# Where two experts' first y tiles and rest rows are scaled out, in a kernel of linear attention and routed experts

## The chip, the cores and the metric

The kernel runs on one core of a Trainium2 chip. The time is device microseconds of one execution, from 3 runs. TensorE multiplies matrices into PSUM (eight banks of 128 x 512 fp32); VectorE and ScalarE do the elementwise work and empty PSUM; SyncE (SP) and ScalarE issue DMAs. Every engine carries out its own list of instructions strictly in order and waits for the others by semaphores.

## The reference

Random-feature linear attention gives x (2304 rows of 512). Each row is sent to one of 8 experts, a two-layer net, and its result is weighted.

```python
q_p, k_p = phi(q_s), phi(k_s)                    # exp of random features
kv = np.einsum('bhsm,bhsd->bhmd', k_p, v)
out = (q_p @ kv) / den                           # -> x, N = 2304, D = 512
logits = x @ w_gate                              # E = 8 experts, F = 1024
expert_idx = np.argmax(logits, axis=1)
gate_w = probs[np.arange(N), expert_idx]
...                                              # rows gathered by expert, at most `capacity`
h = np.maximum(np.einsum('ecd,edf->ecf', disp, w1), 0.0)
y = np.einsum('ecf,efd->ecd', h, w2)
out[i] = gate_w[i] * y[expert_idx[i], pos[i]]
```

## The kernel before

The attention comes first, then the routing, then the experts. The rows lie in four blocks of 576; `item(j)` takes the j-th expert pass over such a block (line 1215). Passes 1 to 3 stand behind branches (line 1443) that are taken only if so many are needed: with these inputs passes 0, 1 and 2 run. "The second expert" below is pass 1, "the third" pass 2 and "the fourth" pass 3, which is prepared but does not run.

Every fp32 product is made of three: each operand is split in a high part (fp32r) and a low part (the remainder), and TensorE adds high x high, low x high and high x low. `split_w_hi` and `hi_part` are casts on ScalarE (line 151), `split_w_lo` and `lo_part` differences on VectorE (line 154). `turn_x` transposes a part of x on VectorE (line 489), and casts and splits it (lines 494, 495).

A pass has two stages. The first makes h = relu(x w1). The second, `second` (`second_late` in the third expert), makes y = h w2 in four tiles of 128 rows and one group of 64 rest rows. A tile is 24 matmuls of 128 x 512: 16 with the high half of w2 (`upper`, lines 1012 and 1013) and 8 with the low half (`lower`, line 1018); the rest rows (line 1022) are 16. The tiles 0 and 2 use PSUM bank 3, the tiles 1 and 3 bank 4, so the fourth tile can only begin when the second has been scaled out of its bank. `second` yields tile 0, the rest rows, tile 1, tile 2, tile 3; `second_late` yields tile 0, tile 1, the rest rows, tile 2, tile 3. After each `yield`, `item` writes what `prep` names for that number n, then `finish`: a scaling by the gate weight on ScalarE (line 1067) into one of three buffers `y`, and the store to the output. For the rest rows it first copies half of the bank on ScalarE (line 1064) and adds the other half on VectorE (line 1065). Stores are issued by SyncE, that of the last tile by ScalarE; each store to the output waits for the one before.

The third expert (`SEVEN`) makes its first stage by seven products of quarters in place of eight (Strassen's scheme in Winograd's form). It needs sums of quarters of w1 (S1 to S4) and of x (T1 to T4), made on VectorE (`sum_part`, line 1114), each split again in high and low. `PREP` names which of this is written into the tail of the second expert, at which n; `BETWEEN` names what is written between the products. The products use, in this order, (A11, B11), (A12, B21), (S2, T2), (S1, T1), (S3, T3), (S4, B22), (A22, T4). S1 and S2 lie in turn in one buffer (`w_sum`); T1 and T2 share one as well.

The order of each engine's list is the order in which this code is written; no scheduler changes it.

Of the kernel before, what the change touches and what calls it, by code (L numbers as in the profile page):

```python
# [29 lines left out]
NB, NBA = SLOTS // 32, 8  # L30
# [28 lines left out]
SEVEN = 2  # L59
# [8 lines left out]
def attention_moe(ctx, tc, kT, qT, va, om, wg, w1, w2, cap, ident, tri, desc, lst, tab0, out):  # L68
# [78 lines left out]
    def split_hi(hi, raw, eng=None):  # L147
        if eng is nc.gpsimd:
            nc.gpsimd.tensor_scalar(hi, raw, 1.0, 1.0, op0=ALU.mult, op1=ALU.mult)
        else:  # L150
            nc.scalar.copy(hi, raw)  # L151

    def split_lo(lo, raw, hi, eng=None):
        (eng or nc.vector).tensor_tensor(lo, raw, hi.bitcast(F32), op=ALU.subtract)  # L154
# [295 lines left out]
    def load_w(i, c, ev, chunks_of="(p k)"):  # L450
        if i == 1:
            f = c // 2 * (FF // 2)
            src = w1[ds(ev, 1), :, f : f + FF // 2].rearrange(f"o {chunks_of} f -> p (o k) f", p=128)
            src = src[:, c % 2 * 2 : c % 2 * 2 + 2, :]
        else:
            src = w2[ds(ev, 1), c * 256 : (c + 1) * 256, :].rearrange("o (k p) f -> p (o k) f", p=128)
        nc.sync.dma_start(w_raw[i][c], src)

    def split_w_hi(i, c, eng=None):
        split_hi(w_hi[i][c], w_raw[i][c], eng)  # L460

    def split_w_lo(i, c, eng=nc.vector, k=None):
        sl, cs = slice(None), slice(None)
        if k is not None:
            sl, cs = slice(k // 2, k // 2 + 1), slice(k % 2 * 256, k % 2 * 256 + 256)
        split_lo(w_lo[i][c][:, sl, cs], w_raw[i][c][:, sl, cs], w_hi[i][c][:, sl, cs], eng)
# [14 lines left out]
    def load_x(rows, b0=0, b1=NB, qs=range(4)):  # L481
        src = x_d[rows, :].rearrange("(b r) (q c) -> q r b c", r=32, q=4)
        for q in qs:
            nc.sync.dma_start(big["xz"][32 * q : 32 * q + 32, b0:b1, :], src[q])


    def turn_x(b0, b1, o=0, eng=nc.vector):
        t = big["xt"][:, o : o + b1 - b0, :].rearrange("p b (k r) -> p b k r", k=4)
        nc.vector.transpose(t, big["xz"][:, b0:b1, :].rearrange("p b (a k) -> p b k a", k=4))
        t = t.rearrange("p b k r -> p k b r")  # L490
        hi, lo = (big[x][:, :, 32 * b0 : 32 * b1].rearrange("p k (b r) -> p k b r", r=32) for x in ("xhi", "xlo"))

        def split():
            nc.scalar.copy(hi, t)
            eng.tensor_tensor(lo, t, hi.bitcast(F32), op=ALU.subtract)

        return split
# [285 lines left out]
    def mm1(f, n, hhi, hlo, hr, nm):  # L783
        xhi, xlo = big["xhi"], big["xlo"]
        fs = slice((f % 4) * 128, (f % 4) * 128 + 128)
        a, z = HALVES[n]
        sl = slice(a, z)
        pt = bank(turn[0] % 3, f"h{nm}{f}{n}")[:, 0 : z - a]
        turn[0] += 1
        for k in range(4):  # L790
            whi_, wlo_ = (w[1][f // 4 * 2 + k // 2][:, k % 2, fs] for w in (w_hi, w_lo))
            nc.tensor.matmul(pt, whi_, xhi[:, k, sl], start=(k == 0), stop=False)  # L792
            nc.tensor.matmul(pt, wlo_, xhi[:, k, sl], start=False, stop=False)  # L793
            nc.tensor.matmul(pt, whi_, xlo[:, k, sl], start=False, stop=(k == 3))  # L794

        def take():
            w = min(z, 4 * SUB) - a
            sl = slice(a, a + w)
            parts = [(hhi[:, f, sl], hlo[:, f, sl], pt[:, 0:w])]
            if n == 1:  # L800
                parts.append((hr[:, f, 0:REST], hr[:, f, REST:], pt[:, w:]))
            for hi, lo, src in parts:
                nc.scalar.activation(hi, src, AF.Relu)  # L803
            for hi, lo, src in parts:
                nc.vector.scalar_tensor_tensor(lo, src, 0.0, hi.bitcast(F32), op0=ALU.max, op1=ALU.subtract)  # L805

        return take
# [77 lines left out]
    for n in range(NK + NT + 3):  # L885
# [9 lines left out]
        elif t < NT:  # L895
            pj = [bank((2 * t + i) % 3, f"pjq{n}{i}") for i in range(2)]
            c = max(i for i in range(len(QB) - 1) if QB[i] <= t)
# [307 lines left out]
    def listing(n):  # L1205
        stop[0] = None
        for _ in range(n):
            if stop[0] is None:
                stop[0] = next(il, 0)
                if stop[0] == 0:  # L1210
                    return
# [3 lines left out]
    def item(j):  # L1215
        nonlocal row, row_a
        nm = f"i{j}"
        last = j == B - 1
        hhi, hlo, hr = h0
        if j > 0:  # L1220
            row_a = nc.scalar.value_load(resd[0:1, 1, j - 1 : j], min_val=0, max_val=N - S)
        out_j = [out[0:SLOTS, :]] * 2 if j == 0 else [out[ds(r, SLOTS), :] for r in (row, row_a)]
        sc = sc_b[:, 0, :] if j == 0 else sc_j[:, j - 1, :]

        def put(i, n, y, out_j=out_j):

            k = int(i == NSUB - 2)
            (nc.sync, nc.scalar)[k].dma_start(out_j[k][i * SUB : i * SUB + n, :], y[0:n, :])

        def addresses():  # L1230
            nonlocal row
            ev = nc.sync.value_load(resd[0:1, 0, j : j + 1], min_val=0, max_val=E - 1)
            row = nc.sync.value_load(resd[0:1, 1, j : j + 1], min_val=0, max_val=N - S)
            evs.append(ev)
            load_x(ds(row, SLOTS))

        def weights():
            for c in range(4):
                load_w(1, c, evs[-1])

        def between(p):
            if p == 1:
                for c in range(4):
                    load_w(2, c, evs[-1])
                addresses()
            for f, *a in BETWEEN.get(p, ()):
                f(*a)
            for c in LOADS.get(p, ()):
                load_w(1, c, evs[-1])

        if j == SEVEN:
            seven(hhi, hlo, hr, nm, between)
        for k, (f, half) in enumerate(STEPS[j > 0] if j != SEVEN else ()):
            mm1(f, half, hhi, hlo, hr, nm)()
            if j == 0:
                listing(5 if k > 4 else 1)
            if 0 < j < B - 1 and k == 0:
                for c in range(4):
                    load_w(2, c, evs[-1])
            if 0 < j and not last and k == 4:  # L1260
                addresses()
                weights()
            if j == 0 and k < 3:
                zero_out(k)
            if half == 0:
                continue
            for i, c in HI_AT[j > 0].get(f, ()):
                split_w_hi(i, c)
            for i, c in LO_AT[j > 0].get(f, ()):
                split_w_lo(i, c)  # L1270
        if j == 0:
            for _ in il:
                pass
            addresses()
            weights()

        def ready(c):
            split_w_hi(1, c)
            split_w_lo(1, c)

        if 0 < j != SEVEN - 1 and not last:
            turn_x(0, NBA)()
            ready(0)
            turn_x(NBA, NB)()
            ready(1)
        if j == B - 2:
            for c in range(4):
                load_w(2, c, evs[-1])
        prep = PREP if j == SEVEN - 1 else {}
        parts = second_late if j == SEVEN else second  # L1290
        for n, (i, pt) in enumerate(parts(hhi, hlo, hr, nm)):
            first_x = turn_x(0, NBA) if j == 0 and n == 1 else None
            for f, *a in prep.get(n, ()):
                f(*a)
            finish(i, pt, nm, sc[:, i : i + 1], put)
            if first_x is not None:
                first_x()
            yield

            if j == 0 and n == 2:  # L1300
                ready(0)
                last_x = turn_x(NBA, NB)
                ready(1)
                last_x()

    def turns(*qs):
        return [(turn_part, q) for q in qs]

    def sums(*qs):
        return [(sum_part, q) for q in qs]  # L1310

    def his(*qs):
        return [(hi_part, q) for q in qs]

    def los(*qs):
        return [(lo_part, q) for q in qs]

    PREP = {
        0: [
            *turns("B11", "B21"), *his("B11", "B21", "A11"), *turns("B12", "B22"), *sums("T1"), *his("T1", "A12"),  # L1320
            *los("B11", "B21", "A11", "A12"), *sums("S1"), *his("S1"), *los("T1"),
        ],
        1: [*sums("T2"), *his("T2"), *los("T2", "S1"), *sums("S2"), *his("S2"), *los("S2"), *sums("S3", "T3", "S4", "T4")],
    }
    BETWEEN = {
        1: [*his("S3", "T3"), *los("S3", "T3")],
# [73 lines left out]


    first = item(0)
    for k in range(BRANCH_AT):
        next(first)
# [98 lines left out]
```

## Time and profile before

| | us |
|---|---|
| median of 3 runs | 268.0 (267.24 to 269.23) |
| profiled execution, whole | 268.11 |
| its span, first to last instruction | 266.3 |
| TensorE busy in the span | 250.7 (94%) |
| VectorE, ScalarE busy | 181.5, 152.5 |
| mean granted clock of TensorE | 0.981 |

The whole time of the profiled execution is 1.8 us above its span. Matmuls are pipelined, so a row's own duration is longer than the distance to the next matmul's start; distances of starts are what counts. Times in the rows are from the span's start.

### The profile page before, as it was taken

What the parts mean: (1) busy time and instruction counts of PE and PEld (TensorE: products, weight loads), DVE (VectorE), ACT (ScalarE), POOL (GpSimd) and SP (SyncE); (2) the same over time, 40 slices, a digit from 0 to 9 for tenths busy, and PEclk for the clock granted to TensorE, in tenths of its full rate; (3) what the DMA queues carried; (4) which work ended last, traced back from release to release, by engine and by line L of the source; (5) the groups of instructions that cost most, each with busy time, mean ns of one, the idle gap of its engine ahead of it and who ended that gap; (6) DMA issues with size and microseconds to landing.
All of it is one profiled execution on the core that took longest, in us unless ns stands there. A gap on an engine that the chain in (4) does not pass through costs nothing. (4 is left out here: it accounts for less than half of the span.)

```text
span 266.3 us, 7692 instructions
## 1 busy us (share of the span) xinstructions
PE 250.7 (94%) x3026; PEld 229.2 (86%) x3026; DVE 181.5 (68%) x385; ACT 152.5 (57%) x383; POOL 52.1 (20%) x102
## 2 busy tenths in 40 slices
PE   8899999999999999999999999999957999999593
PEld 7799898999999999999888899998836999987482
DVE  3988987688899997556836555669880097798400
ACT  4878777899999973256016355534322379703611
POOL 1043212345799964000000000000000000000000
PEclk9999999999999999999999999999995999999799
DMA  6997979326997466920395189900102999062221
GB/s 234 410 304 243 352 254 330 112 100 183 271 259 262 165 206 236 378 74 1 102 287 212 51 278 237 330 6 2 39 0 89 299 248 311 1 214 104 81 62 43
DMA packets 33412, 49.07 MB, mean 184 GB/s; under 512 B 2578, under 2 KB 16530, under 8 KB 33362
## 3 DMA queue, kind: packets, MB, share of 16 engines
q1 hardware_dynamic: 32242, 46.91, 55.9%
q10 hardware_dynamic: 1120, 1.52, 1.7%
q8 instruction: 28, 0.46, 0.7%
q14 instruction: 22, 0.18, 0.2%
HBM read 36.49 MB, written 11.93 MB: 182 GB/s over the span
## 5 line engine op out<-in xcount | busy, mean ns | idle before, releaser
L1012 PE MATMUL yi<-w2hi,hhi 128*128 128x512 f32 x96 | 39.9, 416 | 7.8 <-ACT ysi L1067 7.8
L1013 PE MATMUL yi<-w2hi,hlo 128*128 128x512 f32 x96 | 39.6, 412 | 0.0
L792 PE MATMUL hi<-xhi,w1hi 128*128 128x256 f32 (+1 forms) x128 | 37.8, 295 | 0.0
L793 PE MATMUL hi<-xhi,w1lo 128*128 128x256 f32 (+1 forms) x128 | 37.5, 293 | 0.0
L794 PE MATMUL hi<-xlo,w1hi 128*128 128x256 f32 (+1 forms) x128 | 37.5, 293 | 0.0
L1012 PEld LDWEIGHTS yi<-w2hi,hhi 128*128 128x128 f32 x96 | 19.4, 202 | 12.9 <-ACT ysi L1067 8.7
L805 DVE SCALAR_TENSOR_TENSOR hlo<-hi,hhi 128x256 fp32r<-128x256 f32 x32 | 13.4, 419 | 21.5 <-ACT hr L803 13.9
L206 DVE TENSOR_REDUCE mx<-pjk 128x4 f32<-128x512 f32 (+1 forms) x38 | 23.3, 654 | 4.5 <-PE pjk L189 3.2
L803 ACT ACTIVATE hhi<-hi 128x256 fp32r<-128x256 f32 x32 | 12.2, 386 | 23.9 <-PE hi L794 23.9
L792 PEld LDWEIGHTS hi<-xhi,w1hi 128*128 128x128 f32 x128 | 24.0, 188 | 0.6 <-PE hi L794 0.3
L154 DVE TENSOR_TENSOR w1lo<-w1raw,w1hi 128x1024 fp32r<-128x1024 f32 x11 | 13.3, 1218 | 16.1 <-ACT w1hi L151 16.1
L793 PEld LDWEIGHTS hi<-xhi,w1lo 128*128 128x128 f32 x128 | 24.0, 188 | 0.0
L794 PEld LDWEIGHTS hi<-xlo,w1hi 128*128 128x128 f32 x128 | 24.0, 187 | 0.0
L1018 PE MATMUL yi<-w2lo,hhi 128*128 128x512 f32 x96 | 23.6, 389 | 0.0
L853 ACT ACTIVATE ex<-pjk,mx 128x128 f32<-128x128 f32 x72 | 20.7, 372 | 4.1 <-DVE mx L206 3.4
L1013 PEld LDWEIGHTS yi<-w2hi,hlo 128*128 128x128 f32 x96 | 19.4, 202 | 4.1
L739 PE MATMUL qacc<-kv_sb,qpT 128*64 128x73 f32 x576 | 22.5, 229 | 0.1
L289 PE MATMUL kacc<-v,ex 128*64 128x65 f32 (+1 forms) x576 | 21.4, 230 | 0.7 <-issue 0.7
L1018 PEld LDWEIGHTS yi<-w2lo,hhi 128*128 128x128 f32 x96 | 18.0, 188 | 3.8
L961 ACT ACTIVATE d<-pjq,mx 128x128 f32<-128x128 f32 x72 | 21.1, 411 | 0.2 <-DVE mx L206 0.2
L189 PE MATMUL pjk<-om_s,kraw 64*128 64x128 f32 x288 | 20.4, 284 | 0.8 <-PE pjk L189 0.7
L289 PEld LDWEIGHTS kacc<-v,ex 128*64 128x64 f32 x576 | 19.4, 137 | 2.0 <-issue 1.1
(210 smaller groups left out, 542.7 us busy)
## 6 DMA issues: line engine op xcount, KB each, us to landing
w1raw<-w SPq DMA_DIRECT2D x16, 512.0 KB, 7.0
w2raw<-w SPq DMA_DIRECT2D x16, 512.0 KB, 4.6
x_d<-xr SPq DMA_DIRECT2D x18, 256.0 KB, 3.3
xg<-x_d SPq DMA_DIRECT2D x12, 288.0 KB, 6.1
v<-va SPq DMA_DIRECT2D x8, 325.0 KB, 4.8
kraw<-kT SPq DMA_DIRECT2D x8, 288.0 KB, 4.5
out<-ysi SPq DMA_DIRECT2D x9, 256.0 KB, 2.2
v<-va SPq DMA_DIRECT2D x3, 650.0 KB, 7.2
```

The lines of the kernel that those rows point to most:

```text
L189: nc.tensor.matmul(banks[i][:, k * M : (k + 1) * M], parts[k][rows, :], om_s[rows, :], start=True, stop=True)
L206: nc.vector.tensor_reduce(mx[:, a : a + src.shape[1]], src, op=ALU.max, axis=AX.X, negate=True)
L289: nc.tensor.matmul(acc[f : f + 64, i * 2 * VW + o : i * 2 * VW + o + (z - a) * VW], ex[:, 4 * i + k, f : f + 64], v[:, i, a * VW : z * VW] ...
L739: nc.tensor.matmul(acc[i][r : r + 64, p * ROW : (p + 1) * ROW], qpT[:, r // 64, (4 * i + p) * 64 : (4 * i + p) * 64 + 64], kv_sb[(t * 128 ...
L792: nc.tensor.matmul(pt, whi_, xhi[:, k, sl], start=(k == 0), stop=False)
L793: nc.tensor.matmul(pt, wlo_, xhi[:, k, sl], start=False, stop=False)
L794: nc.tensor.matmul(pt, whi_, xlo[:, k, sl], start=False, stop=(k == 3))
L853: nc.scalar.activation(ex[:, o + k, :], q[:, k * M : (k + 1) * M], AF.Exp, bias=mx[:, o + k : o + k + 1], scale=1.0)
L961: nc.scalar.activation(d[:, 4 + k, :], pj[1][:, k * M : (k + 1) * M], AF.Identity, bias=mx[:, 4 + k : 5 + k], scale=1.0)
L1012: nc.tensor.matmul(pt, hhi[:, f, sl], w2_at(w_hi, f), start=(f == 0), stop=False)
L1013: nc.tensor.matmul(pt, hlo[:, f, sl], w2_at(w_hi, f), start=False, stop=False)
L1018: nc.tensor.matmul(pt, hhi[:, f, sl], w2_at(w_lo, f), start=False, stop=(f == 7))
```

## The change

No instruction is added or taken away. Their order is changed at the ends of the second and the third expert. In the second, S2 and the sums S3, T3, T4 and S4 are written behind the rest rows and the second y tile (n = 3 in place of n = 1), and S1's low half ahead of T2's casts. In the third, the two parts of x and of w1 for the fourth expert were written ahead of all y tiles; they now stand ahead of the rest rows (n = 2) and of the third y tile (n = 3), so that the first two tiles are scaled first.

```diff
@@ -1278,15 +1278,10 @@
             split_w_hi(1, c)
             split_w_lo(1, c)
 
-        if 0 < j != SEVEN - 1 and not last:
-            turn_x(0, NBA)()
-            ready(0)
-            turn_x(NBA, NB)()
-            ready(1)
         if j == B - 2:
             for c in range(4):
                 load_w(2, c, evs[-1])
-        prep = PREP if j == SEVEN - 1 else {}
+        prep = {SEVEN - 1: PREP, SEVEN: STANDARD}.get(j, {})
         parts = second_late if j == SEVEN else second
         for n, (i, pt) in enumerate(parts(hhi, hlo, hr, nm)):
             first_x = turn_x(0, NBA) if j == 0 and n == 1 else None
@@ -1315,12 +1310,21 @@
     def los(*qs):
         return [(lo_part, q) for q in qs]
 
+    def ready_x(*b):
+        turn_x(*b)()
+
+    def ready_w(c):
+        split_w_hi(1, c)
+        split_w_lo(1, c)
+
+    STANDARD = {2: [(ready_x, 0, NBA), (ready_w, 0)], 3: [(ready_x, NBA, NB), (ready_w, 1)]}
     PREP = {
         0: [
             *turns("B11", "B21"), *his("B11", "B21", "A11"), *turns("B12", "B22"), *sums("T1"), *his("T1", "A12"),
-            *los("B11", "B21", "A11", "A12"), *sums("S1"), *his("S1"), *los("T1"),
+            *los("B11", "B21", "A11", "A12"), *sums("S1"), *los("T1"), *his("S1"),
         ],
-        1: [*sums("T2"), *his("T2"), *los("T2", "S1"), *sums("S2"), *his("S2"), *los("S2"), *sums("S3", "T3", "S4", "T4")],
+        1: [*sums("T2"), *los("S1"), *his("T2"), *los("T2")],
+        3: [*sums("S2", "S3"), *his("S2"), *sums("T3", "T4"), *los("S2"), *sums("S4")],
     }
     BETWEEN = {
         1: [*his("S3", "T3"), *los("S3", "T3")],
```

ScalarE, the tail of the second expert, one piece of the difference (`ysi_8719` is its first scaled y tile, `yi1r` the bank of the rest rows, `yi_8653` that of the second tile, `w1hi_1079` here S2's high part):
```order
 L1067 ACTIVATE ysi_8719<-yi_8651,sc_j 128x512
 L151 CAST xhi<-x_more 128x576
+L1064 COPY ysi_8734<-yi1r 64x512
+L1067 ACTIVATE ysi_8734<-ysi_8734,sc_j 64x512
+L1067 ACTIVATE ysi_8747<-yi_8653,sc_j 128x512
 L151 CAST w1hi_1079<-w_sum 128x1024
-L1064 COPY ysi_8741<-yi1r 64x512
-L1067 ACTIVATE ysi_8741<-ysi_8741,sc_j 64x512
-L1067 ACTIVATE ysi_8754<-yi_8653,sc_j 128x512
-L1067 ACTIVATE ysi_8782<-yi_8757,sc_j 128x512
+L1067 ACTIVATE ysi_8782<-yi_8750,sc_j 128x512
 L1067 ACTIVATE ysi_8810<-yi_8785,sc_j 128x512
```
The cast of S2 moves from ahead of the rest rows to behind the second y tile; the two y rows after it differ in a buffer's number alone.

VectorE, the same tail, before, from T2's low half on (`w1lo_1084` is S1's low part, `w1lo_1083` S2's; `w1raw_1075` becomes S3, `x_more` T3, `w1raw_1074` S4, `xt` T4):
```order
L154 TENSOR_TENSOR xlo<-x_more,xhi 128x576
L154 TENSOR_TENSOR w1lo_1084<-w_sum,w1hi_1080 128x1024
L1114 TENSOR_TENSOR w_sum<-w_sum,w1raw_1073 128x1024
L154 TENSOR_TENSOR w1lo_1083<-w_sum,w1hi_1079 128x1024
L1114 TENSOR_TENSOR w1raw_1075<-w1raw_1073,w1raw_1075 128x1024
L1114 TENSOR_TENSOR x_more<-x_more 128x576
L1114 TENSOR_TENSOR w1raw_1074<-w1raw_1074,w_sum 128x1024
L1114 TENSOR_TENSOR xt<-xt,x_more 128x576
L1065 TENSOR_TENSOR ysi_8741<-yi1r,ysi_8741 64x512
```
And in the changed kernel, from S1's low half on:
```order
L154 TENSOR_TENSOR w1lo_1084<-w_sum,w1hi_1080 128x1024
L154 TENSOR_TENSOR xlo<-x_more,xhi 128x576
L1065 TENSOR_TENSOR ysi_8734<-yi1r,ysi_8734 64x512
L1114 TENSOR_TENSOR w_sum<-w_sum,w1raw_1073 128x1024
L1114 TENSOR_TENSOR w1raw_1075<-w1raw_1073,w1raw_1075 128x1024
L1114 TENSOR_TENSOR x_more<-x_more 128x576
L1114 TENSOR_TENSOR xt<-xt,x_more 128x576
L154 TENSOR_TENSOR w1lo_1083<-w_sum,w1hi_1079 128x1024
L1114 TENSOR_TENSOR w1raw_1074<-w1raw_1074,w_sum 128x1024
```
The rest rows' sum (L1065) moves from the last place to the third, ahead of the four sums S2, S3, T3, T4, of S2's low half and of S4's sum.

ScalarE, the tail of the third expert, before (`xhi`, `w1hi_1077` and `w1hi_1078` are the fourth expert's; `yi_9135` and `yi_9136` the banks of the first two y tiles):
```order
L494 CAST xhi<-xt 128x4x256
L151 CAST w1hi_1077<-w1raw_1073 128x1024
L494 CAST xhi<-xt 128x4x320
L151 CAST w1hi_1078<-w1raw_1074 128x1024
L1067 ACTIVATE ysi_9178<-yi_9135,sc_j 128x512
L1067 ACTIVATE ysi_9189<-yi_9136,sc_j 128x512
L1064 COPY ysi_9208<-yi2r 64x512
L1067 ACTIVATE ysi_9208<-ysi_9208,sc_j 64x512
L1067 ACTIVATE ysi_9238<-yi_9213,sc_j 128x512
L1067 ACTIVATE ysi_9266<-yi_9241,sc_j 128x512
```
And in the changed kernel:
```order
L1067 ACTIVATE ysi_9168<-yi_9125,sc_j 128x512
L1067 ACTIVATE ysi_9179<-yi_9126,sc_j 128x512
L494 CAST xhi<-xt 128x4x256
L151 CAST w1hi_1077<-w1raw_1073 128x1024
L1064 COPY ysi_9203<-yi2r 64x512
L1067 ACTIVATE ysi_9203<-ysi_9203,sc_j 64x512
L494 CAST xhi<-xt 128x4x320
L151 CAST w1hi_1078<-w1raw_1074 128x1024
L1067 ACTIVATE ysi_9238<-yi_9208,sc_j 128x512
L1067 ACTIVATE ysi_9266<-yi_9241,sc_j 128x512
```
The first two y tiles move from behind all four casts to ahead of them, and the rest rows to between the two pairs; the third y tile (`yi_9213`, now `yi_9208`) stays behind all of them. On VectorE the rest rows' sum stands correspondingly between the two halves in place of behind both.

## Rows read from the trace of the kernel before

**Rows 1.** Table by stretch, whole core: busy us of each engine, granted clock, DMA.
```profile
150.00:196.50 46.50, 46.50 (x286) 42.65 (x284) 31.14 (x49) 21.01 (x41) 0.00 (x0) 1.00 0.47 134
...
201.15:208.86 7.71, 7.71 (x24) 6.17 (x25) 0.00 (x0) 0.52 (x1) 0.00 (x0) 0.70 0.50 140
...
249.12:256.35 7.23, 7.22 (x24) 5.76 (x25) 1.76 (x2) 1.84 (x3) 0.00 (x0) 0.76 0.29 93
```

**Rows 2.** TensorE in time, end of the second expert: start, us, instruction, [idle before].
```profile
187.43 1.98 PE L1022 MATMUL yi1r<-w2lo,hr 128*128 128x512 f32 x8
...
194.69 1.98 PE L1018 MATMUL yi<-w2lo,hhi 128*128 128x512 f32 x8
201.15 0.80 PE L1012 MATMUL yi<-w2hi,hhi 128*128 128x512 f32 x1 [4.49 <-ACT ysi L1067]
...
208.86 0.29 PE L1138 MATMUL pi<-xhi,w1hi 128*128 128x288 f32 x1
```

**Rows 3.** ScalarE in time, the same stretch.
```profile
193.12 1.05 ACT L151 CAST w1hi<-w_sum 128x1024 fp32r<-128x1024 f32 x1 [3.22 <-DVE w_sum L1114]
194.19 0.58 ACT L1064 COPY ysi<-yi1r 64x512 f32<-64x512 f32 x1
199.66 0.72 ACT L1067 ACTIVATE ysi<-ysi,sc_j 64x512 f32<-64x512 f32 x1 [4.88 <-DVE ysi L1065]
200.41 1.26 ACT L1067 ACTIVATE ysi<-yi,sc_j 128x512 f32<-128x512 f32 x2
```

**Rows 4.** VectorE in time, the same stretch.
```profile
188.31 0.76 DVE L1114 TENSOR_TENSOR x_more<-x_more 128x576 f32<-128x576 f32 x1
...
190.61 1.22 DVE L154 TENSOR_TENSOR w1lo<-w_sum,w1hi 128x1024 fp32r<-128x1024 f32 x1
191.86 1.22 DVE L1114 TENSOR_TENSOR w_sum<-w_sum,w1raw 128x1024 f32<-128x1024 f32 x1
...
198.95 0.68 DVE L1065 TENSOR_TENSOR ysi<-yi1r,ysi 64x512 f32<-64x512 f32 x1
```

**Rows 5.** TensorE in time, end of the third expert.
```profile
231.08 0.39 PE L1012 MATMUL yi<-w2hi,hhi 128*128 128x512 f32 x1
...
238.36 3.79 PE L1018 MATMUL yi<-w2lo,hhi 128*128 128x512 f32 x16
...
243.80 1.98 PE L1022 MATMUL yi2r<-w2lo,hr 128*128 128x512 f32 x8
249.12 0.50 PE L1012 MATMUL yi<-w2hi,hhi 128*128 128x512 f32 x1 [3.35 <-ACT ysi L1067]
...
256.35 0.39 PE L1012 MATMUL yi<-w2hi,hhi 128*128 128x512 f32 x1
...
259.98 1.98 PE L1018 MATMUL yi<-w2lo,hhi 128*128 128x512 f32 x8
```

**Rows 6.** ScalarE in time, the third expert.
```profile
222.71 2.06 ACT L151 CAST w2hi<-w2raw 128x1024 fp32r<-128x1024 f32 x2
...
240.46 1.05 ACT L494 CAST xhi<-xt 128x1024 fp32r<-128x1024 f32 x1 [7.83 <-DVE xt L489]
...
246.28 1.26 ACT L494 CAST xhi<-xt 128x1280 fp32r<-128x1280 f32 x1 [3.83 <-DVE xt L489]
...
262.04 0.69 ACT L1067 ACTIVATE ysi<-yi,sc_j 128x512 f32<-128x512 f32 x1 [4.75 <-PEq L1443]
```

**Rows 7.** VectorE in time, end of the third expert.
```profile
243.81 2.43 DVE L489 STREAM_TRANSPOSE xt<-xg 128x1280 f32<-128x1280 f32 x1
```

**Rows 8.** SyncE's DMA issues in time, third expert.
```profile
205.74 2.25 SPq L457 DMA_DIRECT2D w2raw<-w  x4
...
233.43 3.69 SPq L457 DMA_DIRECT2D w2raw<-w  x4
```

**Rows 9.** The page's part 6: out<-in, engine, xcount, KB each, median us to landing.
```profile
w2raw<-w SPq DMA_DIRECT2D x16, 512.0 KB, 4.6
...
out<-ysi SPq DMA_DIRECT2D x9, 256.0 KB, 2.2
```

## The prediction

> **What bounds the kernel now.** The first view is the table by stretch. From 150 to 196.5 us TensorE is busy all of the time at a granted clock of 1.00, and in two later stretches the mean granted clock is 0.70 and 0.76 [rows 1]. So TensorE sets the pace, and what can be won without taking matmuls away lies where it stands still or runs at the lower of its two levels (1.2 in place of 2.4 GHz). The second view is TensorE's own order in time; it shows two such places, both at the change of experts [rows 2, 5].
>
> *Second expert.* The third y tile's last eight matmuls start at 194.69; the fourth tile's first starts at 201.15, after 4.49 us of waiting for ScalarE's line 1067, the scaling of y [rows 2]. The fourth tile writes the PSUM bank that held the second y tile, and ScalarE empties that bank only at 200.41 [rows 3]: ScalarE is strictly in order, ahead of that scaling stand the cast of S2 (193.12), the copy of the rest rows (194.19) and the scaling of the rest rows (199.66, after 4.88 us of waiting for VectorE), and VectorE reaches the sum of the rest rows only at 198.95, behind all quarter sums and splits of the next expert [rows 3, 4]. The bank itself was ready at about 191, two groups of eight slots after 187.43 [rows 2]. *Third expert.* The same, with other work in front: after the rest rows TensorE waits 3.35 us until 249.12 for line 1067, because ScalarE first turns and splits the x and w1 of a fourth expert (casts at 240.46 and 246.28, the second after 3.83 us of waiting for VectorE) [rows 5, 6]. The trace ends with the third expert's stores; the fourth expert's branch is not taken, so this preparation feeds nothing in this run.
>
> **The size of the two places.** Warm, a y tile's matmul takes a slot of 0.227 us: (259.98 - 256.35) / 16 [rows 5]. Eight take 1.82, a tile of 24 takes 5.44.
> Second expert: the slots end at 194.69 + 1.82 = 196.51, so 201.15 - 196.51 = **4.64 us** stand empty. The tile after the wait runs from 201.15 to 208.86 = 7.71 [rows 2], so the lower clock costs 7.71 - 5.44 = **2.27 us**. Check: a mean clock of 0.70 over 7.71 us is half speed for 4.6 us, a loss of 2.3 [rows 1].
> Third expert: 249.12 - (243.80 + 1.82) = **3.50 us** empty, and 256.35 - 249.12 - 5.44 = **1.79 us** of lower clock [rows 1, 5].
> Together 12.20 us, the most that the change can take away at these places.
>
> **Part 1, the second expert's tail.** No instruction is added or removed; ScalarE now does the rest rows and the second y tile ahead of the cast of S2, and VectorE does the rest rows' sum ahead of the S2, S3, T3, T4, S4 sums and S2's split. I time the new order with the durations of the old. VectorE: the T2 sum starts as before at 188.31 and takes 0.76; S1's low half 1.22 (190.29); T2's low half, of the same width as the sum, 0.76 (191.05); rest rows 0.68, to **191.7** [rows 4]. ScalarE's copy of the rest rows (0.58 [rows 3]) needs the rest rows' matmuls, over at 187.43 + 1.98 = 189.4 [rows 2], and T2's cast ahead of it, which starts at 189.1 and costs no more than the 1.05 us of the wider S2 cast; so it ends by 190.8 and doesn't hold VectorE. Then ScalarE scales the rest rows (0.72) and the second y tile (0.63), to about **193.1** [rows 3]. TensorE wants the bank at 196.51, so 3.4 us are to spare. I take the wait at zero and, with no gap, the clock term at zero too, since the clock is 1.00 all through the gapless 46 us before it [rows 1]. Bounds: 0 if the cover holds, 6.91 back if it doesn't.
>
> The moved work needs a cover too. After 191.7 VectorE has four instructions of 1.22 (the S2, S3 and S4 sums and S2's split, all of one width) and two sums of 0.76: 4 x 1.22 + 2 x 0.76 = 6.4, to about 198 [rows 4]. S2's split is first read by the third of the seven products. A product takes (231.08 - 208.86) / 7 = 3.17 [rows 2, 5]; starting at 196.51 + 5.44 = 201.95, the third product begins at 208.3, 10 us later. S3, S4 and T4 are used later still. Cost: nothing.
>
> **Part 2, the third expert's tail.** In old times (the stage itself moves up by 6.9): the low halves of y tiles one and two start at 238.36, 16 slots, so both are ready by 242.2 and nothing stands ahead of their scaling; two scalings take 1.26 (the x2 row of [rows 3]), to 243.4. Their banks are then free, and TensorE wants the first at 245.62. Behind them come the cast of x (1.05 [rows 6]) and of w1 (1.05), and VectorE's two low halves (1.22 each, the width of [rows 4]), to about 246.9; the rest rows are ready at 243.80 + 1.98 = 245.8, their sum ends at 246.9 + 0.68 = 247.6, the second transposition (2.43 [rows 7]) at 250.0, its cast (1.26) and the w1 cast at 252.3; then the third y tile is scaled, by 253.1. TensorE's last tile ends at 245.62 + 2 x 5.44 = 256.5, and its scaling follows it as it does now at 262.04 [rows 6]. Margin 3.4 us. The wait goes, and what is late next is TensorE's own last tile. Value: -5.29; bounds 0 and 5.29.
>
> **DMA and queues.** SP moves earlier with the scaled tiles: the second expert's stores stand ahead of the third expert's w2 loads, issued at 205.74 [rows 8]. Even if these did not move, the last is issued by 207.99 and lands 4.6 later [rows 9], at 212.6, and the cast that reads the first moves from 222.71 [rows 6] to 215.8. Nothing is lost. The first stores of the third expert move from 249 to about 234, close behind the four w2 loads for the fourth expert, issued from 233.43 on [rows 8]; that is priced as rival D.
> The Trainium skill's page "DMA: Bandwidth & Descriptors" (Issuing engines are not separate DMA queues) says that transfers share the same 16 engines and interleave; by that rule those stores would be slower than the 2.2 us of the page's row. No row of before has a store in that place.
>
> **The sum.** 4.64 + 2.27 + 3.50 + 1.79 = 12.20 off the profiled execution's 268.11 (span 266.3) is **255.9 us**. The median of the shown runs is 268.0, so the two stand alike.
> One rule weighs against the clock terms. The rows give 4.06 us for them, 1.5% of the span. The Trainium skill's page "TensorE: Matmul & The Clock Gate" (What's actually happening) says that for modelling the ramp penalty is under 1% of a typical kernel's span; by that rule the two terms would be at most 2.7 and the time 257.3. The measured slots differ from it here, and the sum goes by them.
>
> **Rivals.**
> A. *Only one place is freed* (0.05): 268.11 - 6.91 = 261.2, or 262.8 with the other. For the second expert it needs the chain over VectorE to be 3.4 us later than worked out, over a chain of some 5 us (188.3 to 193.1); for the third, the banks of y tiles one and two not to be free by 245.62. Against it: every duration is from a row of the same instruction.
> B. *The change doesn't do what it says* (0.03): the waits named are those of a store or of another engine, and return; about 268. Against it: TensorE starts within 0.2 us after ScalarE's scaling, both times [rows 2, 3].
> C. *The waits go, the lower clock stays* (0.03): 255.9 + 4.06 = 260.0. Against it, the 46 us at 1.00 without a gap.
> D. *Slower through the stores* (0.02). Each store to the output waits for the one before. From 234.1 on (new times) four stores in a row must land before the last one, which is ready at 250.4; up to (250.4 - 234.1) / 4 = 4.1 us each, nothing is lost. At 7.1 each the whole gain is gone, and beyond some 7.8 the kernel is over 1% slower. For it: the w2 loads just ahead of them. Against: stores landed in 2.2 us as a median [rows 9], the loads are over after the first two stores, and the third isn't ready before about 241.
>
> **How the numbers follow.** The forecast, both places freed, has a chance of 0.87. Its own spread: downward the shown runs' spread (1.23 above the median, taken both ways), 254.7. Upward rival C nearly, or some 3.5 us of the 12.2 left in small waits, 259.5. That leaves out most of A, B and D, about one in ten, and some of C. A change of 1% (2.7 us, about what a measurement of this kernel tells from none) is reached by the forecast, A and C: faster 0.95; within 1% 0.03 (B); slower 0.02 (D).
>
> **What would show it.** Right: in TensorE's order in time no gap between the third and fourth y tile of the second expert, nor after the rest rows of the third; no 0.43 us slots there and a granted clock of 1.00; the seven products starting near 202, the last y tile ending near 250; ScalarE scaling the second y tile by 193 and then waiting for TensorE. Wrong: a new wait of TensorE for line 1067 or for S2's split, or the last scaling of the kernel not directly behind the last matmul. A VectorE that runs its sums slower beside ScalarE's scalings would make the first number wrong; a late landing of the fourth expert's w1, which now stands ahead of the third y tile's scaling, the second.

## The result, and the profile after

The changed kernel takes 256.12 us (median of 4 runs, 255.6 to 259.23), the kernel before 267.62 (median of 4, the three shown and one more, 266.82 to 269.23). The ratio is 0.9587, with an interval of 0.9498 to 0.9677: 4.1% faster. The profiled execution takes 256.34 us (span 254.6, mean granted clock 0.997); 255.9 was forecast, in a range from 254.7 to 259.5.

TensorE in time in the changed kernel (start, us, instruction), to be held against [rows 2, 5]:
```profile
187.30 1.98 PE L1022 MATMUL yi1r<-w2lo,hr 128*128 128x512 f32 x8
...
194.55 1.98 PE L1018 MATMUL yi<-w2lo,hhi 128*128 128x512 f32 x8
196.37 0.39 PE L1012 MATMUL yi<-w2hi,hhi 128*128 128x512 f32 x1
...
201.81 0.29 PE L1138 MATMUL pi<-xhi,w1hi 128*128 128x288 f32 x1
...
231.31 3.79 PE L1018 MATMUL yi<-w2lo,hhi 128*128 128x512 f32 x16
...
236.75 1.98 PE L1022 MATMUL yi2r<-w2lo,hr 128*128 128x512 f32 x8
238.57 0.39 PE L1012 MATMUL yi<-w2hi,hhi 128*128 128x512 f32 x1
...
244.01 0.39 PE L1012 MATMUL yi<-w2hi,hhi 128*128 128x512 f32 x1
...
247.63 1.97 PE L1018 MATMUL yi<-w2lo,hhi 128*128 128x512 f32 x8
```
The second expert's fourth tile starts at 196.37, one slot group (1.82) after 194.55, and carries no wait; it takes 201.81 - 196.37 = 5.44. After the third expert's rest rows the next tile starts at 238.57, again 1.82 after the group before, and takes 244.01 - 238.57 = 5.44. Both waits and both slow tiles are gone. The table by stretch says the same of the clock (columns as in [rows 1]):
```profile
186.00:196.50 10.50, 10.50 (x48) 8.71 (x47) 10.47 (x13) 5.13 (x7) 0.00 (x0) 1.00 0.19 62
196.50:202.00 5.50, 5.50 (x27) 4.56 (x26) 0.71 (x1) 0.69 (x1) 0.00 (x0) 1.00 0.54 188
...
225.00:239.00 14.00, 14.00 (x63) 11.60 (x62) 10.52 (x16) 4.08 (x6) 0.00 (x0) 1.00 0.56 189
```

ScalarE in time in the changed kernel, first the second expert's tail, then the third's (compare [rows 3, 6]):
```profile
189.79 0.58 ACT L1064 COPY ysi<-yi1r 64x512 f32<-64x512 f32 x1
191.36 0.72 ACT L1067 ACTIVATE ysi<-ysi,sc_j 64x512 f32<-64x512 f32 x1 [0.99 <-DVE ysi L1065]
192.11 0.69 ACT L1067 ACTIVATE ysi<-yi,sc_j 128x512 f32<-128x512 f32 x1
192.70 1.04 ACT L151 CAST w1hi<-w_sum 128x1024 fp32r<-128x1024 f32 x1
...
235.14 0.69 ACT L1067 ACTIVATE ysi<-yi,sc_j 128x512 f32<-128x512 f32 x1 [1.12 <-PE yi L1018]
...
244.72 0.69 ACT L1067 ACTIVATE ysi<-yi,sc_j 128x512 f32<-128x512 f32 x1
249.69 0.69 ACT L1067 ACTIVATE ysi<-yi,sc_j 128x512 f32<-128x512 f32 x1 [4.28 <-issue]
```
The second y tile is scaled by 192.80, 3.57 us before its bank is wanted at 196.37. In the third expert the second tile is scaled by 235.83, right behind its matmuls, and the third tile by 245.41, behind the fourth expert's casts, 4.3 us ahead of the last.

VectorE in time, the same kernel (compare [rows 4]):
```profile
190.65 0.68 DVE L1065 TENSOR_TENSOR ysi<-yi1r,ysi 64x512 f32<-64x512 f32 x1
...
195.99 1.21 DVE L1114 TENSOR_TENSOR w1raw<-w1raw,w_sum 128x1024 f32<-128x1024 f32 x1
```
The rest rows' sum starts at 190.65 where it was at 198.95, and the last of the moved sums ends at 197.2, 11 us before the third product (201.81 + 2 x 3.17 = 208.2).

### The profile page after: what moved, and what is told of

It reads as the page before. It is cut to its first block, busy times and chain, and to the rows that moved or that the text cites. A ratio compares the mean times of both kernels' runs of the same rounds, so it can differ in the third digit from the quotient of the medians.

```text
span 254.6 us, 7692 instructions
## 1 busy us (share of the span) xinstructions
PE 247.1 (97%) x3026; PEld 228.0 (90%) x3026; DVE 181.5 (71%) x385; ACT 152.8 (60%) x383; POOL 52.2 (21%) x102
## 4 chain that ended last, share of the span: by engine, by line
PE 90%; DVE 3%; issue 2%; ACT 2%; POOL 0%; ACTq 0%; POOLq 0%; DVEq 0%
PE qacc L739 8%; PE yi L1012 8%; PE yi L1013 8%; PE pjk L189 8%; PE yi L1018 8%; PE pjq L189 7%; PE kacc L289 7%; PE hi L792 6%; PE hi L793 6%; PE hi L794 6%; PE qtr L916 4%; PE pi L1139 3%; PE pi L1140 3%; PE pi L1138 3%; PE yi1r L1022 1%
## 5 line engine op out<-in xcount | busy, mean ns | idle before, releaser
L1012 PE MATMUL yi<-w2hi,hhi 128*128 128x512 f32 x96 | 37.4, 390 | 0.0
L1013 PE MATMUL yi<-w2hi,hlo 128*128 128x512 f32 x96 | 37.4, 389 | 0.0
L803 ACT ACTIVATE hhi<-hi 128x256 fp32r<-128x256 f32 x32 | 12.2, 386 | 24.0 <-PE hi L794 24.0
L189 PE MATMUL pjk<-om_s,kraw 64*128 64x128 f32 x288 | 21.6, 296 | 0.6 <-PE pjk L189 0.6
L1012 PEld LDWEIGHTS yi<-w2hi,hhi 128*128 128x128 f32 x96 | 18.0, 188 | 3.7
L1013 PEld LDWEIGHTS yi<-w2hi,hlo 128*128 128x128 f32 x96 | 18.0, 188 | 3.6
L945 POOL TENSOR_TENSOR d<-d,mx 128x512 f32<-128x512 f32 x18 | 18.7, 1040 | 11.9 <-DVE mx L206 6.8
L739 PEld LDWEIGHTS qacc<-kv_sb,qpT 128*64 128x64 f32 x576 | 19.9, 136 | 1.4 <-PE qtr L916 0.2
```

What stands on the lines that cost most here:

```text
L189: nc.tensor.matmul(banks[i][:, k * M : (k + 1) * M], parts[k][rows, :], om_s[rows, :], start=True, stop=True)
L739: nc.tensor.matmul(acc[i][r : r + 64, p * ROW : (p + 1) * ROW], qpT[:, r // 64, (4 * i + p) * 64 : (4 * i + p) * 64 + 64], kv_sb[(t * 128 ...
L945: nc.gpsimd.tensor_tensor(d[:, 0:4, :], d[:, 0:4, :], spread(mx, 0), op=ALU.add)
L1012: nc.tensor.matmul(pt, hhi[:, f, sl], w2_at(w_hi, f), start=(f == 0), stop=False)
L1013: nc.tensor.matmul(pt, hlo[:, f, sl], w2_at(w_hi, f), start=False, stop=False)
```

## The experiments

The theory: each of the two places is a wait for a PSUM bank, and costs the time that TensorE stands still plus what the clock that falls from it takes; the moved work costs nothing as long as the bank is free in time. Six kernels test it, and a seventh tries a further step.

**One place at a time.** In `e1_second_only` the block that prepared the fourth expert is put back; in `e2_third_only` the old `PREP` (its second line is shown, cut at its end).
```diff
e1:  +        if 0 < j != SEVEN - 1 and not last:
     +            turn_x(0, NBA)()
     ...
     -        prep = {SEVEN - 1: PREP, SEVEN: STANDARD}.get(j, {})
     +        prep = {SEVEN - 1: PREP}.get(j, {})
e2:  ...
     -        1: [*sums("T2"), *los("S1"), *his("T2"), *los("T2")],
     -        3: [*sums("S2", "S3"), *his("S2"), *sums("T3", "T4"), *los("S2"), *sums("S4")],
     +        1: [*sums("T2"), *his("T2"), *los("T2", "S1"), *sums("S2"), *his("S2"), *los("S2"), ...],
```


> The new order in the second expert's tail alone; the third expert's tail as before. If each place is a wait for a PSUM bank with its own price, this takes 4.64 + 2.27 = 6.9 us from the kernel before: about 261 us, no gap after the second expert's third y tile, and the gap of 3.5 us after the third expert's rest rows still there with the clock falling behind it. Rival, one gap is only passed on to the next place: the second gap grows by several us and the time stays above 265.

> The new order in the third expert's tail alone; the second expert's tail as before. Two separate places: 3.50 + 1.79 = 5.3 us from the kernel before, about 262.5 us, with the gap of 4.6 us in the second expert still there. Rival, the places hang together: a gain clearly off 5.3, so that this and the other half don't add up to the 11.5 of the whole change.

Measured: e1 261.75 us (4 runs, 261.07 to 262.19), ratio to the kernel before 0.9781 (0.9735 to 0.9828); e2 262.13 (4 runs, 261.9 to 263.07), 0.9801 (0.9752 to 0.9851). The kernel before, beside them, 267.8. TensorE in time, the one place that each keeps, e1:
```profile
237.09 1.97 PE L1022 MATMUL yi2r<-w2lo,hr 128*128 128x512 f32 x8
242.42 0.79 PE L1012 MATMUL yi<-w2hi,hhi 128*128 128x512 f32 x1 [3.35 <-ACT ysi L1067]
...
253.07 1.97 PE L1018 MATMUL yi<-w2lo,hhi 128*128 128x512 f32 x8
```
and e2:
```profile
194.44 1.98 PE L1018 MATMUL yi<-w2lo,hhi 128*128 128x512 f32 x8
200.90 0.50 PE L1012 MATMUL yi<-w2hi,hhi 128*128 128x512 f32 x1 [4.48 <-ACT ysi L1067]
...
253.90 1.97 PE L1018 MATMUL yi<-w2lo,hhi 128*128 128x512 f32 x8
```
The waits that stay are those of before (4.49 and 3.35), to 0.01 us. Neither is passed on, and the other place of each is free: e1's last tile of the second expert starts at 196.71, 1.81 behind the eight matmuls at 194.90, and e2's third tile of the third expert at 244.83, 1.81 behind those at 243.02.

The medians fall by 6.1 and 5.7, where 6.9 and 5.3 were forecast; the intervals, 4.6 to 7.1 and 4.0 to 6.6 us, hold the forecasts and tell no more. Together it is 11.7, where the whole change gives 11.5. The traces are sharper. From the rest rows' second half to the last eight matmuls it was 259.98 - 187.43 = 72.55 us [rows 2, 5]; it is 253.07 - 187.64 = 65.43 in e1 and 253.90 - 187.19 = 66.71 in e2, so 7.12 and 5.84 less. What goes beyond 6.91 and 5.29 is a lower price in clock at the place that stays (last section). The two places are separate and add up.

**The waits filled.** `e3_filled_waits` is the kernel before, with matmuls in the waits whose result nothing reads.
```diff
+    def fill(nm, at, n):
+        if nm == at:
+            pt = bank(0, f"fill{nm}")
+            for k in range(n):
+                nc.tensor.matmul(pt, h0[0][:, k % 8, 0:SUB], w2_at(w_hi, k % 8), start=True, stop=True)
...
+        fill(nm, "i2", 15)     # ahead of the third expert's third y tile
...
+            if i == NSUB - 2:
+                fill(nm, "i1", 20)     # ahead of the second expert's fourth y tile
```


> The kernel before with matmuls that feed nothing put into the two waits (20 ahead of the second expert's last y tile, 15 ahead of the third expert's third), in a PSUM bank that is free; 20 and 15 slots of 0.227 are 4.54 and 3.41 us, just under the waits of 4.64 and 3.50. If the lower clock is a consequence of TensorE's standing still, the waits stay (the last scaling that frees the bank comes no earlier) but the y tiles behind them take 5.44 in place of 7.71 and 7.23: 4.1 us less, about 263.5. Rival, the clock falls there for another reason: the tiles stay at 0.43 us a slot and the time at 267.6.

Measured: 264.16 us (9 runs, 263.66 to 266.42), ratio 0.9882 (0.9852 to 0.9911), 3.6 below the 267.8 beside it. TensorE in time, and the table by stretch over the two filled waits and the tiles behind them:
```profile
195.99 4.69 PE L1028 MATMUL filli<-w2hi,hhi 128*128 128x512 f32 x20
200.66 0.50 PE L1012 MATMUL yi<-w2hi,hhi 128*128 128x512 f32 x1
...
204.42 1.98 PE L1018 MATMUL yi<-w2lo,hhi 128*128 128x512 f32 x8
...
246.52 0.50 PE L1012 MATMUL yi<-w2hi,hhi 128*128 128x512 f32 x1
...
250.27 1.98 PE L1018 MATMUL yi<-w2lo,hhi 128*128 128x512 f32 x8
```
```profile
195.95:200.60 4.65, 4.65 (x21) 3.57 (x20) 3.19 (x5) 1.40 (x3) 0.00 (x0) 1.00 0.00 0
200.60:206.24 5.64, 5.64 (x25) 4.62 (x25) 0.00 (x0) 0.59 (x2) 0.00 (x0) 1.00 0.37 116
242.95:246.50 3.55, 3.55 (x16) 2.64 (x15) 2.22 (x3) 2.83 (x4) 0.00 (x0) 1.00 0.00 0
246.50:252.10 5.60, 5.60 (x26) 4.62 (x26) 1.78 (x2) 1.85 (x3) 0.00 (x0) 1.00 0.27 98
```
The bank comes no earlier than before, and yet the tiles behind now run at 1.00. They take 204.42 + 1.82 - 200.66 = 5.58 us and 250.27 + 1.82 - 246.52 = 5.57, in place of 7.71 and 7.23: 3.8 us less (4.1 forecast). So the lower clock at these places is a consequence of TensorE's standing still, and the change's gain divides into about 8.1 us of waits and 3.8 of clock.

**The dead work taken away.** `e4_no_fourth` is the changed kernel without the fourth expert's turns and splits, which nothing uses with these inputs.
```diff
-        prep = {SEVEN - 1: PREP, SEVEN: STANDARD}.get(j, {})
+        prep = {SEVEN - 1: PREP}.get(j, {})
```


> The changed kernel without the fourth expert's turns and splits (its loads stay, and its branch isn't taken with these inputs). If only the place of that work mattered, its removal changes nothing now: 256 us, TensorE's order in time the same to 0.2 us, and about 12 us less VectorE and 4.4 us less ScalarE work in the third expert's tail. Rival, the amount of work beside the matmuls costs too (slower scalings, or the last scaling late): 0.5 us or more less.

Measured: 255.83 us (4 runs, 255.03 to 256.75), ratio to the kernel before 0.9558 (0.9506 to 0.9611); the changed kernel's 0.9587 lies within. The stretch from 231 to 247 us of e4:
```profile
231.00:247.00 16.00, 16.00 (x72) 13.23 (x72) 1.07 (x3) 3.38 (x5) 0.00 (x0) 1.00 0.37 126
```
and of the changed kernel:
```profile
231.00:247.00 16.00, 16.00 (x73) 13.23 (x72) 10.37 (x9) 7.48 (x9) 0.00 (x0) 1.00 0.39 133
```
VectorE does 9.3 us less there (the 12 of the expectation were added up wrongly), ScalarE 4.1 less, and TensorE is busy for all 16.00 us either way. The medians, 0.3 us apart with an interval of over 1 us to each side, can't tell the rival's 0.5 from none; the traces can. From the rest rows' second half to the last eight matmuls it is 247.60 - 187.27 = 60.33 us in e4 and 247.63 - 187.30 = 60.33 in the changed kernel. So the work cost by its place alone.

**The edge.** `e5_edge` and `e6_over_edge` move pieces back ahead of the rest rows until the cover is used up (the new lines alone are shown).
```diff
e5:  +        1: [*sums("T2"), *los("S1"), *his("T2"), *los("T2"), *sums("S2"), *his("S2"), *sums("S3"), *los("S2")],
     +        3: [*sums("T3", "T4", "S4")],
e6:  +        1: [... as e5, *sums("T3", "S4")],
     +        3: [*sums("T4")],
```


> The changed kernel with four pieces moved back ahead of the rest rows: the S2 and S3 sums and S2's two splits. VectorE's rest rows then start three slots of 1.13 us later, near 194.0 in place of 190.65, and the second y tile is scaled by 196.2, when the bank is wanted at 196.4. If cover is all that counts, no gap and 256 us. Rival, the moved work costs by itself: 1 us or more of it shows.

> The same with the T3 and S4 sums ahead of the rest rows as well, another 0.67 + 1.14 us: the second y tile is scaled by 198.0, and TensorE waits about 1.7 us from 196.4 on. By the price of the waits alone the time is 1.7 us above the changed kernel, about 258, at a clock of 1.00. If a gap of this length lowers the clock as those of 4.6 and 3.5 us did, some 1.8 to 2.3 us more, about 260.

Measured, one run each: e5 256.21 us, e6 258.67. ScalarE and TensorE in time in e5:
```profile
196.16 0.69 ACT L1067 ACTIVATE ysi<-yi,sc_j 128x512 f32<-128x512 f32 x1
```
```profile
195.12 1.98 PE L1018 MATMUL yi<-w2lo,hhi 128*128 128x512 f32 x8
196.94 0.46 PE L1012 MATMUL yi<-w2hi,hhi 128*128 128x512 f32 x1
```
The bank is free at 196.85 and wanted at 195.12 + 1.82 = 196.94: 0.1 us of cover left, and no wait. TensorE in e6:
```profile
194.87 1.98 PE L1018 MATMUL yi<-w2lo,hhi 128*128 128x512 f32 x8
198.45 0.50 PE L1012 MATMUL yi<-w2hi,hhi 128*128 128x512 f32 x1 [1.60 <-ACT ysi L1067]
...
202.23 1.98 PE L1018 MATMUL yi<-w2lo,hhi 128*128 128x512 f32 x8
```
and its clock, us by us:
```profile
197.00:198.00 1.00, 0.00 (x0) 0.00 (x0) 0.60 (x1) 0.97 (x2) 0.00 (x0) 1.00 0.00 0
198.00:199.00 1.00, 0.55 (x2) 0.48 (x3) 0.00 (x0) 0.98 (x2) 0.00 (x0) 1.00 0.09 20
199.00:200.00 1.00, 1.00 (x6) 0.80 (x5) 0.00 (x0) 0.00 (x0) 0.00 (x0) 1.00 0.53 111
```
1.81 us more of VectorE work ahead of the rest rows gives 198.45 - (194.87 + 1.82) = 1.76 us of standstill (1.7 forecast). The clock stays at 1.00, from 200 to 204 us too, and the tile takes 202.23 + 1.82 - 198.45 = 5.60: this gap costs its own length and 0.16 us, no more. From the rest rows to the last eight matmuls e6 takes 249.87 - 187.62 = 62.25 us, 1.92 above the changed kernel's 60.33; what else parts 258.67 from 256.12 lies outside that stretch.

**A further step.** The end of the kernel behind the last matmul is the only part that TensorE doesn't set now.
```diff
-        w = DM // 2 if nm == f"i{B - 1}" and i == NSUB - 2 else DM
+        w = DM // 2 if nm in ("i2", "i3") and i == NSUB - 2 else DM
```


> The changed kernel with the third expert's last y tile scaled half on ScalarE and half on VectorE, as the code does for the fourth. With TensorE gapless, the tail behind its last matmul is all that is left at the end: the scaling of 0.69 us falls to about 0.4, 0.3 us less, about 255.8; that is under what the measurement tells from none, so the trace's distance from the last matmul to the last store's issue decides (0.8 us now, 0.5 then). Rival, the tail is the store alone: no difference there either.

Measured: 256.35 us (5 runs, 256.23 to 256.53), ratio to the kernel before 0.9589 (0.9563 to 0.9614), as the changed kernel. The trace shows why, TensorE, ScalarE and VectorE in time:
```profile
247.69 1.97 PE L1018 MATMUL yi<-w2lo,hhi 128*128 128x512 f32 x8
```
```profile
249.75 0.47 ACT L1067 ACTIVATE ysi<-yi,sc_j 128x256 f32<-128x256 f32 x1 [4.28 <-issue]
250.77 0.35 ACTq L1228 DMA_DIRECT2D out<-ysi  x1
```
```profile
250.26 0.48 DVE L1069 TENSOR_SCALAR ysi<-yi,sc_j 128x256 f32<-128x256 f32 x1 [3.80 <-ACT ysi L1067]
```
Both expectations fail: VectorE waits until ScalarE is done, so the halves, 0.47 and 0.48, stand one behind the other, and the store is issued 250.77 - (247.69 + 1.97) = 1.1 us after the last matmul in place of 0.8. Whether two halves at the same time would help was not tried. No version here is clear of the changed kernel.

## Why the prediction was right

**The places and their size.** From the rest rows' second half to the first product it was 208.86 - 187.43 = 21.43 us [rows 2] and is 201.81 - 187.30 = 14.51: 6.92 less, 6.91 forecast (4.64 + 2.27). From there to the last eight matmuls it was 259.98 - 208.86 = 51.12 [rows 2, 5] and is 247.63 - 201.81 = 45.82: 5.30 less, 5.29 forecast (3.50 + 1.79). e1 and e2 show that each part of the change gives its own share, e3 that the clock terms belong to the waits. The agreement to 0.01 us says less than it seems to: the prices were read from this same trace of before, and in the trace of after both tiles run at the full clock. The price in clock differs from trace to trace (1.74 for 2.27 in e2, 1.59 for 1.79 in e1), so a sum from another trace of the kernel before could have been some tenths of a microsecond off.

**The cover.** Forecast for the second expert: rest rows' sum over at 191.7, second tile scaled by 193.1; measured 191.33 and 192.80. The cover of 3.4 us was 3.57, and e5 and e6 use it up where the durations say. For the third: the third tile scaled by 253.1 in old times, 246.2 in new; measured 245.41, so the margin of 3.4 us was 4.3. There VectorE was not what came last, as I had it: it waited 0.23 us for ScalarE's copy of the rest rows. I had let both scalings begin only when both tiles were ready; the first ran earlier.

**The sum.** 12.2 us were forecast off the profiled execution, 11.8 are gone (268.11 to 256.34). The rest lies behind the last matmuls: from their start to the end of the span it was 266.3 - 259.98 = 6.3 us and is 254.6 - 247.63 = 7.0; against that the second expert's tail begins 0.13 earlier. In the seven experiments this piece is 6.1 to 6.9 long, whatever was changed, and its last part is the landing of the last store. From that store's issue to the end of the span it was 266.3 - 262.76 = 3.5 us and is 254.6 - 250.41 = 4.2, with 3.3 to 4.2 in the seven experiments, and no engine has a row in it; so the 0.7 lie behind the issue. I take them for that store's own spread; it was not tried by itself. The tail was a term that I had left as it was.

**The rule on the clock.** The Trainium skill's page "TensorE: Matmul & The Clock Gate" (What's actually happening) has the ramp under 1% of a typical kernel's span; taken over to the two terms, that gave 257.3. The page says it of the warm-up at a kernel's start, and here the slow slots stand behind two gaps in the middle: they took 4.06 us, 1.5%, and e3 gets 3.8 back with nothing else won. The rows were the better guide.

**The rivals.** A (one place only) and B (another wait) are refuted by the after trace and by e1 and e2; C (the clock stays low) by the 1.00 in the stretches above, and by e3 for the reason. D, the chain of stores, exists, and did not decide. SyncE's issues in the third expert's tail of the changed kernel:
```profile
234.04 0.38 SPq L1228 DMA_DIRECT2D out<-ysi  x1
...
237.17 0.37 SPq L1228 DMA_DIRECT2D out<-ysi  x1
...
240.85 0.53 SPq L1228 DMA_DIRECT2D out<-ysi  x1
...
245.44 0.34 SPq L1228 DMA_DIRECT2D out<-ysi  x1
```
The second store, ready at 235.83, goes out at 237.17, so the first held it for 3.1 us, more than the 2.2 of [rows 9]. The prediction had these stores close behind w2 loads issued from 233.43 on, but that is the loads' old time beside the stores' new one: the loads move up too, are issued from 226.38, and the first store follows 7.7 us later.

The loads still run then. In the half microsecond behind the first store's issue the DMA engines move 393 GB/s in the changed kernel, 397 in e6 and 389 in e7, and the second store goes out 3.13, 2.99 and 3.19 us behind the first. In e2, e4 and e5 the rate is lower there, 238 to 287, and the distance 2.29 to 2.46; in the kernel before and in e1 nothing moves, and it is 2.27 and 2.30. That agrees with what the page "DMA: Bandwidth & Descriptors" of the Trainium skill (Issuing engines are not separate DMA queues) says of transfers that share the engines; no run takes the loads away by themselves. The third and fourth go out as soon as they are scaled, so 3.1 stays under the 4.1 per store at which the chain would have begun to cost.

One of the four runs of the changed kernel took 259.23 us at a clock of 1.00; there is no trace of it, and what it waited for stays open.

## What to carry to other kernels

Where one engine is nearly always busy and an in-order helper both empties its buffers and prepares the next stage, look up for each buffer when it is ready, when it is emptied and when it is wanted again; work that isn't needed until later belongs behind the emptying, and costs nothing as long as the emptying ends before the buffer is wanted and the moved work itself before its own reader. Work out that cover from the rows of before: here it was right to 0.2 us in the second expert and 0.9 too small in the third, and adding up the durations told both where the wait begins (e5) and how long it gets (e6). A gap in the matmuls has a second price in the clock, which was about half the gap at two places and almost nothing at a shorter one, and shows behind it, in the slots of the following tile.

## What I had not expected of the hardware

A gap's price in clock does not follow its length simply. In the kernel before, the gap of 4.64 us cost 2.27 in the tile behind it; in e2 the same gap, equal to 0.01 us, cost 7.18 - 5.44 = 1.74 (the tile from 200.90 to 208.08). The moment differed too: in the kernel before the clock falls at about 199, two microseconds ahead of the next matmul (0.95 from 198 to 199, 0.50 from 199 to 200), in e2 only behind it (1.00 until 201, 0.66 from 201 to 202). The gap of 3.50 cost 1.79, in e1 7.03 - 5.44 = 1.59. The one of 1.76 in e6 cost 0.16, at a clock of 1.00. A price read from one trace is therefore one case of several; the mean granted clock of the kernel before went from 0.977 to 0.987 from run to run. And the clock can fall after the work has begun again: in the kernel before, TensorE resumes at 249.12 [rows 5] at full clock and drops to the lower level only in the following microsecond, as the table by stretch shows:
```profile
249.00:250.00 1.00, 0.88 (x4) 0.74 (x5) 1.00 (x2) 0.97 (x3) 0.00 (x0) 1.00 0.03 12
250.00:251.00 1.00, 1.00 (x4) 0.78 (x3) 0.88 (x2) 0.26 (x1) 0.00 (x0) 0.55 0.69 258
251.00:252.00 1.00, 1.00 (x4) 0.76 (x3) 0.00 (x0) 0.72 (x1) 0.00 (x0) 0.50 0.02 8
```
